# Attention and two Strassen-style products on one core: GpSimd's sums given to VectorE, six places for raw words, another order at pair changes

## The chip, the core and the metric

The kernel runs on one core of a Trainium2 chip. Its engines are TensorE (PE, matmuls; PEld is its weight load), VectorE (DVE), ScalarE (ACT), GpSimd (POOL) and SyncE (SP), which here only issues DMAs; ACT issues DMAs too. Each engine takes its instructions in the order in which they were written. The metric is the device time of one execution in microseconds (us), as the median of several runs.

## The reference, cut to what matters

```python
def _attn_ref(q, k, v, p):             # batch 8, heads 8, seq 576, head_dim 64; 32 packed rows
    p_packed = sm_attn(p, k, v)        # softmax(p k^T / 8) v
    return sm_attn(q, p_packed, p_packed)

def _moe_ref(x, w1, w2, w3, w_out):    # x: 4608 x 512, w1, w2: 512 x 1024
    return ((x @ w1) * (x @ w2)) @ w3 @ w_out

def _moe2_ref(x, w_in, w_out):         # w_in: 512 x 2048, w_out: 2048 x 512
    h = x @ w_in
    g = np.where(h >= 1, h, np.where(h <= -1, 0.0, (h + 1) ** 2 / 4))
    return g @ w_out
```

The output of attention is the input of the first product chain, and that chain's output is the input of the second.

## The kernel before

All big matmuls take each operand as two parts, a high part (an ACT copy into the matmul's own fp32r type) and a remainder (value minus high part, a subtract on DVE or POOL), and make three products of them (`PASSES`). The work has three stages.

**Stage one** (to about 620 us of the trace) does attention and the first chain, batch by batch (`b`). Within a batch, 16 `ab_unit`s (L378) and 8 `x2_unit`s (L402) follow each other on PE; attention of the next batch is spread between them, and after every unit one item of `weight_tasks` (L576) is run, which prepares the weights of the second chain: `convert` turns 64-bit words into float32 (ACT and three DVE instructions), `combine` (L637) adds two 128x512 quarters on POOL, and `part` (L626) makes the high part on ACT and the remainder on POOL and stores both to DRAM.

**Stage two** (about 620 to 1028 us) is x @ w_in as a Strassen-Winograd product with seven products (A11, S1, S2, A12, S4, S3, A22). The columns of x come in five pairs of halves (`PAIRS`): four of 512 columns and a last one of 256. A pair has eight steps `s`; a step runs the seven products of six matmuls on PE, the A22 of a step only after S1 of the next one. ACT copies the bank of A11 to `m1`, of S1 to `m5` and of S2 to `u2`, because S2, S4 and S3 add onto those banks; DVE adds them back (L869: `U` twice, `L` once). `upper` and `lower_*` put the piecewise square on the results (ACT: L809, L812; DVE: L815), and form the differences U2 = U1 - U0 (L837, end of `upper`) and two planes of `L` (`lower_end`, L858); SP stores all to DRAM (`gd`) for stage three. While a pair runs, the seven right sides of the next pair are made by eleven tasks (`x2_tasks`, L662): seven `parts` (ACT copy L672, DVE remainder L673 into one of nine `x2s` tiles) and four `combine`s (POOL, L667, in place in the tile `f`). Tables set where they run: `MID` (after A12 of step i), `LAST` (after S3) and `END` (after `upper`). Before the change, S4 and S3 of the next pair come in END of step 7, and its A22 in END of step 0, that is when that pair already runs.

**Stage three** (from about 1028 us) is g @ w_out in the same scheme: 5 pairs x 7 products x 4 entries `j`. An entry loads a tile of raw words (`raw`, 128x1024 floats for the wide pairs, 512 KB) by SP (L924), makes high part (ACT, L941) and remainder (DVE, L942) in one of five `op` tiles, and PE runs 12 matmuls on it (L1050). An entry of A22 needs two raw tiles, subtracted in place first (`g_combine`, POOL, L933). At entry x the program makes the parts of entry x + 3, fills free raw places with loads (`g_load`), and subtracts for entry x + 5 if that is of A22. There are four raw places (`RAWS`). After the fourth entry of a product `evacuate` takes its two banks out: A11, S1, S2 and A22 by ACT copies (L1023), A12, S3 and S4 by DVE adds (L1027).

```python
    def g_combine(x):
        if x < len(seq) and seq[x][1] == A22:
            a, b = rawg[x]
            nc.gpsimd.tensor_tensor(out=a, in0=a, in1=b, op=ALU.subtract)
...
        g_parts(x + AHEAD)
        g_load()
...
        g_combine(x + AHEAD + 2)
```

The activation's scratch tiles are those of tag `r` ([128, 2, 512], two of them): the relu and its square stand there in stage two, and nothing uses them after it.

## Time and profile before

| | |
|---|---|
| three runs | 1438.79 us median (1434.61 to 1439.05) |
| the profiled execution | 1430.22 us, of it 1428.4 us span from the first to the last instruction |
| PE busy | 1308.1 us (92% of the span) |
| DVE busy | 849.6 us (59%) |
| ACT busy | 676.0 us (47%) |
| POOL busy | 206.7 us (14%) in 134 instructions |
| chain that ended last | PE 53%, DVE 17%, DMA 14%, ACT 9%, POOL 2% |
| granted clock of PE, mean | 0.971 of full speed |

The busy shares are means over three stages with different limits. Of a stretch, read first how long PE was busy in it and at which granted clock, then what its waits ended on. The profiled execution is 8.6 us shorter than the median of the runs. Raw loads were 128 DMAs, right sides' and weights' POOL work stands in stages one and two, and the POOL subtracts of stage three are 20.

### The profile page before, as it was taken

How to read it: one execution, taken by the hardware profiler on the slowest of the kernel's cores; microseconds unless marked ns; L12 is line 12 of the kernel's file. 1: busy time of each engine (PE TensorE's matmuls, PEld its weight loads, DVE VectorE, ACT ScalarE, POOL GpSimd, SP SyncE). 2: the span in 40 equal slices, each digit the busy share in tenths (PEclk: the TensorE clock that was granted, in tenths of full speed). 3: DMA queues.
4: the chain of work that ended last, by engine and by line, in shares of the span. 5: the costliest groups of instructions: out<-in, count | busy, mean ns of one | idle time of the engine just before them, and what ended most of it. 6: DMA issues, size and time to landing. Idle time of an engine off the chain costs nothing.

```text
span 1428.4 us, 21147 instructions
## 1 busy us (share of the span) xinstructions
PE 1308.1 (92%) x8184; PEld 1072.7 (75%) x8184; DVE 849.6 (59%) x1334; ACT 676.0 (47%) x1144; POOL 206.7 (14%) x134
## 2 busy tenths in 40 slices
PE   6689799999999999989989899898879899998988
PEld 2366578879888898968767687787767687877877
DVE  4684576658676766617767777666634544444533
ACT  3344244445545454426656667565533443425333
POOL 0000032333233232201101020000001102020011
PEclk9799999999999999989999999999999999999999
DMA  8763465557555533178566565567898666666665
GB/s 278 233 218 104 143 214 193 173 186 232 200 182 196 203 141 145 50 281 323 211 228 213 206 237 196 207 216 266 275 343 351 240 216 236 220 218 228 223 201 164
DMA packets 122900, 306.78 MB, mean 215 GB/s; under 512 B 10160, under 2 KB 44976, under 8 KB 117680
## 3 DMA queue, kind: packets, MB, share of 16 engines
q1 hardware_dynamic: 85904, 236.09, 47.8%
q10 hardware_dynamic: 36896, 69.35, 13.6%
q8 instruction: 64, 1.05, 0.3%
q14 instruction: 36, 0.29, 0.1%
HBM read 199.36 MB, written 106.04 MB: 214 GB/s over the span
## 4 chain that ended last, share of the span: by engine, by line
PE 53%; DVE 17%; DMA 14%; ACT 9%; issue 4%; POOL 2%; ACTq 1%; SPq 0%; POOLq 0%; DVEq 0%
PE psk L402 11%; PE x L1050 10%; PE psk L378 8%; PE x L801 7%; DMA raw<-g 6%; PE z L801 3%; PE z L1050 3%; PE y L1050 3%; DVE op L942 2%; ACT r L809 2%; ACT r L812 2%; PE psk L486 2%; DMA raw<-w3T 2%; PE y L801 2%; DVE U L815 2%
## 5 line engine op out<-in xcount | busy, mean ns | idle before, releaser
L942 DVE TENSOR_TENSOR op<-raw,op 128x1024 fp32r<-128x1024 f32 (+1 forms) x140 | 161.3, 1188 | 182.8 <-ACT op L941 182.1
L402 PEld LDWEIGHTS psk<-g,w 128*128 128x128 f32 x1500 | 200.3, 188 | 28.4 <-ACT st L429 17.7
L378 PE MATMUL psk<-at,m 128*128 128x288 f32 x1494 | 214.3, 298 | 5.0 <-DVE at L329 1.9
L378 PEld LDWEIGHTS psk<-at,m 128*128 128x128 f32 x1494 | 200.7, 188 | 19.7 <-issue 9.5
L941 ACT ACTIVATE op<-raw 128x1024 fp32r<-128x1024 f32 (+1 forms) x140 | 130.3, 968 | 173.9 <-POOL raw L933 76.8
L402 PE MATMUL psk<-g,w 128*128 128x288 f32 x1500 | 209.1, 297 | 3.8 <-ACT st L429 3.3
L626 POOL TENSOR_TENSOR hl<-cvx,hl 128x512 fp32r<-128x512 f32 x56 | 73.9, 1319 | 447.6 <-ACT hl L625 411.6
L1050 PE MATMUL x<-op,w 128*128 128x512 f32 (+1 forms) x480 | 111.5, 388 | 25.2 <-ACT op L941 13.9
L801 PE MATMUL x<-x2s,wi 128*128 128x512 f32 (+1 forms) x480 | 120.0, 387 | 7.4 <-ACT m L865 6.9
L1050 PEld LDWEIGHTS x<-op,w 128*128 128x128 f32 x480 | 87.5, 197 | 48.5 <-ACT op L941 17.1
L801 PEld LDWEIGHTS x<-x2s,wi 128*128 128x128 f32 x480 | 87.9, 197 | 29.4 <-ACT m L865 10.4
L390 DVE TENSOR_TENSOR tb<-psk,ta 128x288 f32<-128x288 f32 x124 | 56.3, 454 | 86.3 <-ACT ta L388 61.8
L809 ACT ACTIVATE r<-U,half 128x1024 f32<-128x1024 f32 (+1 forms) x40 | 42.7, 1067 | 126.8 <-DVE U L869 126.8
L933 POOL TENSOR_TENSOR raw<-raw,raw 128x1024 f32<-128x1024 f32 (+1 forms) x20 | 43.8, 2190 | 404.6 <-DMA raw<-g 338.6
L667 POOL TENSOR_TENSOR f<-f 128x1024 f32<-128x1024 f32 (+1 forms) x20 | 43.7, 2186 | 361.2 <-DVE x2s L673 360.8
L104 DVE TENSOR_TENSOR g<-tb,g 128x288 fp32r<-128x288 f32 x128 | 91.6, 716 | 3.4 <-ACT g L103 2.8
L815 DVE SCALAR_TENSOR_TENSOR U<-U,r 128x512 f32<-128x512 f32 (+1 forms) x80 | 58.9, 777 | 53.1 <-ACT r L812 53.1
L801 PE MATMUL x<-x2s,ws 128*128 128x512 f32 (+1 forms) x240 | 62.3, 395 | 19.4 <-ACT x2s L672 8.0
L812 ACT ACTIVATE r<-r 128x1024 f32<-128x1024 f32 (+1 forms) x80 | 78.0, 975 | 2.5
L1050 PE MATMUL x<-op,hwi 128*128 128x512 f32 (+1 forms) x360 | 77.3, 373 | 0.0
L486 PE MATMUL psk<-wo,w3f 128*128 128x512 f32 x128 | 62.9, 644 | 13.9 <-DVE w3f L135 13.9
L124 ACT ACTIVATE cvt<-raw 128x512 f32<-128x512 f32 x72 | 48.4, 675 | 54.1 <-DMA raw<-w 25.9
(112 smaller groups left out, 2040.7 us busy)
## 6 DMA issues: line engine op xcount, KB each, us to landing
raw<-g SPq DMA_DIRECT2D x128, 512.0 KB, 4.9
g<-L SPq DMA_DIRECT2D x32, 1024.0 KB, 4.1
ws<-ws ACTq DMA_DIRECT2D x38, 512.0 KB, 4.3
g<-U SPq DMA_DIRECT2D x64, 256.0 KB, 2.0
w<-hl ACTq DMA_DIRECT2D x28, 512.0 KB, 3.0
x2d<-st ACTq DMA_DIRECT2D x72, 144.0 KB, 2.6
wi<-hl ACTq DMA_DIRECT2D x20, 512.0 KB, 5.1
qk<-kT SPq DMA_DIRECT2D x8, 1152.0 KB, 9.1
```

The costliest lines, as they stand in the source:

```text
L104: nc.vector.tensor_tensor(out=dst[:, 1], in0=src, in1=dst[:, 0].bitcast(F32), op=ALU.subtract)
L378: nc.tensor.matmul(ps[w][:, :HS], m_tile[b, w, n][:, s, G, c0 * P:(c0 + 1) * P], at_tile[b][:, G, v, hf * HS:(hf + 1) * HS], start=(k == 0 ...
L402: nc.tensor.matmul(ps, w34[kt][:, s, mt * P:(mt + 1) * P], g_t[kt, hf][:, v, :], start=(kt == kts[0] and n == 0), stop=(kt == kts[-1] and ...
L486: nc.tensor.matmul(acc[4 * hf + m], w3f[hf, j][:, m * P:(m + 1) * P], wof[j], start=(j == 0), stop=(j == 7))
L626: nc.gpsimd.tensor_tensor(out=lo, in0=q[a], in1=hi.bitcast(F32), op=ALU.subtract)
L801: nc.tensor.matmul(bank[s, b][:, :N], w, x2_t[t, q][:, m, k, :N], start=(j == 0 and q in (A11, S1, A12)), stop=(j == 5), skip_group_check= ...
L809: nc.scalar.activation(out=r, in_=h, func=AF.Relu, scale=0.5, bias=half)
L812: nc.scalar.activation(out=r, in_=r, func=AF.Square)
L815: nc.vector.scalar_tensor_tensor(out=out, in0=h, scalar=1.0, in1=r, op0=ALU.max, op1=ALU.min)
L941: nc.scalar.activation(out=o[:, :, 0, :N], in_=a[0], func=AF.Copy)
L942: nc.vector.tensor_tensor(out=o[:, :, 1, :N], in0=a[0], in1=o[:, :, 0, :N].bitcast(F32), op=ALU.subtract)
L1050: nc.tensor.matmul(bank[b][d][:, :N], w2_t[q][j // 2][:, 2 * (j % 2) + k, s, d * P:(d + 1) * P], op[x][:, k, v, :N], start=start and k == ...
```

## The change

Every tensor instruction of POOL goes to DVE, in its place in program order: the 56 remainders and 32 sums of `weight_tasks`, the 20 `combine`s of `x2_tasks` and the 20 of `g_combine`. The raw ring gets six places; the two new ones are the two `r` tiles. The first four entries are loaded as before (`g_load(4)`), the next loads come after the stores of the last step. In `x2_tasks` the last combine writes to quarter 11 instead of 21 and stands ahead of the parts of A12. The subtract that ended `upper` becomes `upper_end`. At a pair change (step 0 of the next pair) the tasks S4, S3 and A22 run after A11, after S1 and after A12 of that step, and `upper_end` and `lower_end` of the step before run only after S3.

```diff
-                    nc.gpsimd.tensor_tensor(out=lo, in0=q[a], in1=hi.bitcast(F32), op=ALU.subtract)
+                    nc.vector.tensor_tensor(out=lo, in0=q[a], in1=hi.bitcast(F32), op=ALU.subtract)
...
-                return lambda: nc.gpsimd.tensor_tensor(out=q[d], in0=q[a], in1=q[b], op=op)
+                return lambda: nc.vector.tensor_tensor(out=q[d], in0=q[a], in1=q[b], op=op)
...
-            return lambda: nc.gpsimd.tensor_tensor(out=x2f[dst], in0=x2f[a], in1=x2f[b], op=ALU.subtract)
+            return lambda: nc.vector.tensor_tensor(out=x2f[dst], in0=x2f[a], in1=x2f[b], op=ALU.subtract)
...
-            parts(S2, 11), parts(A12, 21), combine(21, 21, 11), parts(S4, 22), parts(S3, 12), parts(A22, 21),
+            parts(S2, 11), combine(11, 21, 11), parts(A12, 21), parts(S4, 22), parts(S3, 12), parts(A22, 11),
...
+        store(s, G11, 1, h[:, 0:1, :N])
+
+    def upper_end(s):
+        N = PAIRS[s // 8][1]
+        h = kept[s, 0]
         nc.vector.tensor_tensor(out=h[:, 2, :N], in0=h[:, 1, :N], in1=h[:, 0, :N], op=ALU.subtract)
-        store(s, G11, 1, h[:, 0:1, :N])
         store(s, GT1, 1, h[:, 2:3, :N])
...
-    RAWS, OPS = 4, 5
+    RAWS, OPS = 6, 5
...
     def raw_tile(n):
-        return ring("raw", n, [P, 2, 512], F32)
+        return buf("r") if n > 3 else ring("raw", n, [P, 2, 512], F32)
...
-            nc.gpsimd.tensor_tensor(out=a, in0=a, in1=b, op=ALU.subtract)
+            nc.vector.tensor_tensor(out=a, in0=a, in1=b, op=ALU.subtract)
...
-    MID = {2: 2, 3: 1, 4: 1, 5: 1, 7: 1}
+    MID = {2: 2, 3: 1, 4: 1, 5: 1, 7: 1, 0: 1}
     LAST = {7: 2}
-    END = {7: 2, 0: 1}
...
         if s:
             lower_begin(s - 1)
+        tasks(1 if i == 0 else 0)
         product(s, S1)
...
             ws_load(s + 1, nc.scalar)
+        tasks(1 if i == 0 else 0)
         product(s, S2)
...
-        if s:
+        if s and i:
             lower_end(s - 1)
...
+        if s and i == 0:
+            upper_end(s - 1)
+            lower_end(s - 1)
         tasks(LAST.get(i, 0))
         if s + 1 < steps:
             upper(s)
-            tasks(END.get(i, 0))
+            if i < 7:
+                upper_end(s)
...
-            for n in range(RAWS):
+            for n in range(4):
                 tiles["raw", n] = raw_tile(n)
-            g_load()
+            g_load(4)
...
     lower_end(steps - 1)
     flush_stores()
+    g_load()
```

What this does to the order of instructions is shown at three places. Names are those of the program; a number behind one tells buffers apart, and x, y, z are PE's banks.

The first is ACT in step 0 of the second pair, the pair change (`m` is m1 or m5, `u` is u2, `x2s` a right side). Before, from the square of step 7's `upper` on:

```order
L812 ACTIVATE r<-r 128x1024
L672 ACTIVATE x2s<-f 128x1024 x2
L865 ACTIVATE m_8526<-x 128x512
L809 ACTIVATE r<-L,half 128x512
L865 ACTIVATE m_8537<-z 128x512
L809 ACTIVATE r<-x,half 128x512
L812 ACTIVATE r<-r 128x1024
L752 DMA ws<-ws_74 128x1024
L865 ACTIVATE u_8557<-x 128x512
L809 ACTIVATE r<-U,half 128x1024
L812 ACTIVATE r<-r 128x1024
L672 ACTIVATE x2s<-f 128x1024
```

ACT in the same place after the change:

```order
L812 ACTIVATE r<-r 128x1024
L869 ACTIVATE m_8518<-x 128x512
L809 ACTIVATE r<-L,half 128x512
L672 ACTIVATE x2s<-f 128x1024
L869 ACTIVATE m_8532<-z 128x512
L809 ACTIVATE r<-x,half 128x512
L812 ACTIVATE r<-r 128x1024
L752 DMA ws<-ws_74 128x1024
L672 ACTIVATE x2s<-f 128x1024
L869 ACTIVATE u_8555<-x 128x512
L672 ACTIVATE x2s<-f 128x1024
L809 ACTIVATE r<-U,half 128x1024
```

The copies for S4 and S3 moved from ahead of m1 to behind it, one of them ahead of m5 and one ahead of u2; the copy for A22 moved from behind `upper` of step 0 to ahead of it.

The second is DVE in step 2 of the first pair, where the program makes the first right side of the next pair (L673, remainder) and the first combine. Before:

```order
L869 TENSOR_TENSOR U<-y,m_7441 128x512
L858 TENSOR_TENSOR L<-L,U 128x1024
L673 TENSOR_TENSOR x2s<-f,x2s 128x1024
L869 TENSOR_TENSOR U<-z,u_7472 128x512
L869 TENSOR_TENSOR L<-x,m_7452 128x512
```

DVE in the same place after the change:

```order
L873 TENSOR_TENSOR U<-y,m_7441 128x512
L862 TENSOR_TENSOR L<-L,U 128x1024
L673 TENSOR_TENSOR x2s<-f,x2s 128x1024
L667 TENSOR_TENSOR f<-f 128x2x512
L873 TENSOR_TENSOR U<-z,u_7472 128x512
L873 TENSOR_TENSOR L<-x,m_7452 128x512
```

The combine, POOL's before, now stands on DVE ahead of the two adds that take PE's banks.

The third is DVE around the A22 entries of the second pair in stage three (`U<-z` and `L<-x` are `evacuate` of S4 and S3). Before:

```order
L1027 TENSOR_TENSOR L<-x,L 128x512 x2
L942 TENSOR_TENSOR op_11290<-raw_11222,op_11290 128x2x512
L942 TENSOR_TENSOR op_11307<-raw_11240,op_11307 128x2x512
L942 TENSOR_TENSOR op_11327<-raw_11272,op_11327 128x2x512
L942 TENSOR_TENSOR op_11347<-raw_11310,op_11347 128x2x512
L1027 TENSOR_TENSOR U<-z,U 128x512 x2
L942 TENSOR_TENSOR op_11369<-raw_11330,op_11369 128x2x512
L942 TENSOR_TENSOR op_11389<-raw_11350,op_11389 128x2x512
```

DVE in the same place after the change (`r` is a raw place in an activation's scratch tile):

```order
L1038 TENSOR_TENSOR L<-x,L 128x512 x2
L946 TENSOR_TENSOR op_11294<-raw_11190,op_11294 128x2x512
L937 TENSOR_TENSOR raw_11242<-raw_11242,raw_11244 128x1024
L946 TENSOR_TENSOR op_11311<-raw_11207,op_11311 128x2x512
L937 TENSOR_TENSOR r<-r 128x1024
L946 TENSOR_TENSOR op_11331<-raw_11242,op_11331 128x2x512
L937 TENSOR_TENSOR raw_11314<-raw_11314,raw_11316 128x1024
L946 TENSOR_TENSOR op_11351<-r,op_11351 128x2x512
L937 TENSOR_TENSOR raw_11334<-raw_11334,raw_11336 128x1024
L1038 TENSOR_TENSOR U<-z,U 128x512 x2
L946 TENSOR_TENSOR op_11373<-raw_11314,op_11373 128x2x512
L946 TENSOR_TENSOR op_11393<-raw_11334,op_11393 128x2x512
```

The four subtracts of raw words (L937, POOL's L933 before) now stand between the remainders, each two entries ahead of the remainder that uses it, all of them ahead of the two adds that empty S4's banks.

## Rows read from the trace of the kernel before

**Rows 1.** Busy time by stretch: us, engines' busy time, PEclk, DMA share, GB/s

```profile
core 0: us, PE busy (x) PEld busy (x) DVE busy (x) ACT busy (x) POOL busy (x), PEclk, DMA share, GB/s
180.00:606.00 426.00, 414.09 (x3787) 368.44 (x3786) 291.20 (x538) 209.93 (x481) 128.25 (x92) 1.00 0.51 176
705.00:990.00 285.00, 264.19 (x1130) 211.09 (x1129) 198.23 (x267) 177.62 (x240) 26.74 (x13) 0.96 0.62 217
1100.00:1428.00 328.00, 299.81 (x1414) 245.80 (x1412) 147.03 (x142) 122.34 (x150) 43.80 (x20) 0.98 0.64 216
713.00:726.00 13.00, 9.96 (x42) 7.38 (x40) 10.83 (x13) 8.88 (x12) 2.35 (x1) 1.00 0.48 162
```

**Rows 2.** Waits of PE from 1100 us on: us in total, times, longest

```profile
PE x L1050 <- ACT op L941: 13.9, 9, 3.8
PE x L1050 <- DVE op L942: 11.2, 12, 2.4
```

**Rows 3.** The same from 1100 to 1125 us, the first A22 run

```profile
PE x L1050 <- DVE op L942: 4.5, 2, 2.4
PE x L1050 <- ACT op L941: 2.5, 2, 1.6
```

**Rows 4.** Timeline of the third A22 run: start, us, engine, [idle before <-releaser]

```profile
1276.39 1.06 ACT L941 ACTIVATE op<-raw 128x1024 fp32r<-128x1024 f32 x1 [7.92 <-POOL raw L933]
...
1285.84 2.34 POOL L933 TENSOR_TENSOR raw<-raw,raw 128x1024 f32<-128x1024 f32 x1 [6.97 <-DMA raw<-g]
...
1289.32 0.49 PE L1050 MATMUL x<-op,w 128*128 128x512 f32 x1 [3.78 <-ACT op L941]
```

**Rows 5.** The page's DMA issues: count, KB, median us from issue to landing

```profile
raw<-g SPq DMA_DIRECT2D x128, 512.0 KB, 4.9
```

**Rows 6.** Waits of PE from 705 to 990 us, the four pair changes

```profile
PE x L801 <- ACT x2s L672: 8.0, 4, 2.5
PE x L801 <- ACT m L865: 6.2, 6, 1.5
PE x L801 <- DVE x2s L673: 6.2, 4, 1.7
```

**Rows 7.** Timeline of the first pair change, ACT and PE

```profile
713.29 1.99 ACT L672 ACTIVATE x2s<-f 128x1024 fp32r<-128x1024 f32 x2
...
715.81 1.66 PE L801 MATMUL x<-x2s,wi 128*128 128x512 f32 x6 [1.52 <-ACT m L865]
...
718.43 0.58 ACT L865 ACTIVATE u<-x 128x512 f32<-128x512 f32 x1
...
720.12 1.56 PE L801 MATMUL x<-x2s,wi 128*128 128x512 f32 x6
...
726.31 0.50 PE L801 MATMUL x<-x2s,ws 128*128 128x512 f32 x1 [1.83 <-ACT x2s L672]
...
728.55 2.50 PE L801 MATMUL x<-x2s,ws 128*128 128x512 f32 x5 [1.74 <-DVE x2s L673]
```

**Rows 8.** Timeline, steps 2, 3 and 5 of the second pair

```profile
746.92 1.22 DVE L673 TENSOR_TENSOR x2s<-f,x2s 128x1024 fp32r<-128x1024 f32 x1
...
750.93 0.58 ACT L865 ACTIVATE m<-x 128x512 f32<-128x512 f32 x1
...
751.77 1.56 PE L801 MATMUL x<-x2s,wi 128*128 128x512 f32 x6
...
771.70 1.67 PE L801 MATMUL x<-x2s,wi 128*128 128x512 f32 x6 [0.17 <-ACT m L865]
```

**Rows 9.** DVE groups by form, 180 to 606 us: count, busy us, mean ns, idle before

```profile
L104 DVE TENSOR_TENSOR g<-tb,g 128x288 fp32r<-128x288 f32 x112 | 84.4, 754 | 0.0
L390 DVE TENSOR_TENSOR tb<-psk,ta 128x288 f32<-128x288 f32 x112 | 50.8, 454 | 72.3 <-ACT ta L388 55.5 <-PE psk L378 10.0 <-ACT g L103 6.5
L104 DVE TENSOR_TENSOR m<-psk,m 128x512 fp32r<-128x512 f32 x50 | 32.2, 685 | 31.4 <-ACT m L103 31.4
```

**Rows 10.** The page's costliest groups: POOL's remainders of weights in stage one

```profile
L626 POOL TENSOR_TENSOR hl<-cvx,hl 128x512 fp32r<-128x512 f32 x56 | 73.9, 1319 | 447.6 <-ACT hl L625 411.6
```

More of the change, by code (lines that the diff above doesn't have):

```diff
@@ L1006, in fused_kernel @@
     upper(steps - 1)
+    upper_end(steps - 1)
     lower_begin(steps - 1)
```

## Prediction

> **What bounds the kernel now.** First the busy time by stretch [rows 1]. In 180 to 606 us, most of stage one, PE is busy 414 of 426 us at a granted clock of 1.00: there is little to win. In the pair changes of stage two (705 to 990 us) it is busy 264 of 285 us at 0.96, and from 1100 us on 300 of 328 us at 0.98. So the sum is made of what PE loses in these two stretches, by standing still and by running at the lower of its two clock levels (1.2 of 2.4 GHz).
>
> Next who PE waits for. From 1100 us on it waits 13.9 us for high parts and 11.2 us for remainders [rows 2], 25.1 us, all at the entries of A22 (five runs of four); 7.0 us of it in the first run [rows 3]. The timeline of the third run shows why [rows 4]: POOL's subtract had been waiting for a raw load, ACT for POOL, PE for ACT. The lower clock costs 328 x 0.02 = 6.6 us more. In stage two PE waits 8.0 + 6.2 + 6.2 = 20.4 us at four pair changes [rows 6]. The first change shows the three stops [rows 7]: 1.52 us at S2 of step 0 (ACT copied two right sides from 713.29 us, m1 came behind them), 1.83 and 1.74 us at A22 (its right side is made behind `upper`). That is 5.1 us a change. The clock costs 285 x 0.04 = 11.4 us.
>
> **Part 1, A22 in stage three.** An entry of A22 holds two raw places, so with four places two entries are on their way. One needs a load of 4.9 us [rows 5], POOL's 2.34 us and ACT's 1.06 us [rows 4], and a DVE remainder of 1.22 us (same shape in [rows 8]): 9.5 us for two entries, 4.8 us each. PE needs 2.9 us for twelve matmuls: three products of six took 4.31 us from 715.81 to 720.12 [rows 7]. With six places three entries are on their way, and the subtract takes DVE's 1.22 us: 4.9 + 1.22 + 1.06 + 1.22 = 8.4 us for three, 2.8 us each. That is just under PE's pace, so I let the stops of the three middle runs go entirely. In the first run the loads share the DMA engines with stage three's weights; I keep 3 of its 7.0 us. In the last run entries are half as long, but a load is not half as quick; I keep 1.3 us. Gain 25.1 - 4.3 = 20.8 us, with ends at 12 (half of it) and 25.1. Of the 6.6 us of low clock I count 5 as gained, since a run that stops for 3 us may still have it.
>
> The change adds a wait: DVE now waits for the raw load itself. Behind the subtract for entry x + 5 stand the remainder of the entry ahead of it and, at the fourth subtract, the two adds that empty S4's banks; PE waits for both. The third A22 entry can be loaded only when the remainders of S4's last two entries free its places, so DVE stands about 3 us there. What hides this is the two finished `op` tiles that PE then still has, 2 x 2.9 = 5.8 us. Without that cover it would cost those 3 us in each of five runs, 15 us.
>
> **Part 2, the pair change.** ACT has ten instructions from `upper` of step 7 to u2 in either order, so u2 still ends near 719.0 us (718.43 + 0.58, [rows 7]). m1 now comes where the copies began, at 713.29 us, so S2 can start on time, at 715.81 - 1.52 = 714.3 us, and S3 three products later, at 718.6 us. But S3 needs u2 and its right side's remainder. The copy for that now comes just ahead of u2 and ends about 718.4 us; on DVE the two `smaller` of the old pair (0.69 us each, [rows 9]) stand in front, then the remainder takes its 1.22 us: it ends between 719.7 and 720.4 us. S3 started at 720.12 us before. So the first stop isn't gained, it moves from S2 to S3 (1.1 to 2.2 us). A22's right side is ready by then, and A22 starts three products behind S3: the two later stops, 3.57 us, go. Three changes: 10.7 us. At the fourth the new products have 256 columns while ACT and DVE still work on 512 of the old pair; I count 1.3 of its 5.1 us. `upper_end` and `lower_end` of step 7 come later, behind the adds; their stores have a step of time until their buffers are needed, so I cost that at nothing; if the stores were late, DVE's add would wait about 1 us a change.
>
> **Part 3, inside a pair.** Four combines of 1.22 us a pair go from POOL to DVE. In step 2 the remainder ends at 748.1 us, then come the add, `upper` and m1, which ends at 751.51 us; S2 starts at 751.77 [rows 8]. The slack is 0.26 us, and a combine of 1.14 us (1.22 less the overlap of neighbours) stands now between: a stop of 0.9 us. ACT then runs late, and each of the next three tasks adds about 0.5 us; one of them shows 0.17 us already [rows 8]. That is 2.2 us a pair, for three pairs 6.6 us lost; the fourth prepares a pair of half the width, where I see none.
>
> **The clock in stage two.** Of its 11.4 us I take 9 as additional to the stops, and give back 7.5, because the stops that remain are shorter and stand alone: in 713 to 726 us, where the only stop was 1.52 us, the clock stayed at 1.00 [rows 1, 7]. The ends are 0 and 9.
>
> **Part 4, stage one.** 88 instructions of POOL (56 of 1.32 us [rows 10], 32 sums alike) become DVE instructions of 0.69 us [rows 9]: 60.7 us. But POOL's work slows DVE. The remainder of g, with both inputs in SBUF, takes 754 ns on average; the product of the same length just before it, with an input in PSUM, takes 454 ns [rows 9]. That is 112 x 0.30 = 33.6 us which come back. DVE goes from 291 to 318 of 426 us, 75%. I count 0 us, between 3 us of gain (stretched instructions in PE's path get shorter) and 22 us of loss (below). The Trainium skill, "SBUF — State Buffer", section "SBUF: two separate sides", says that a GpSimd instruction and a DVE one with two SBUF inputs exclude each other, the loser blocked for the whole instruction. By it alone every POOL instruction could hold up DVE for its 1.3 us, 88 x 1.3 = 114 us, and DVE would have less to do after the change; by the row it has 27 us more. The measured 33.6 us stays.
>
> **The sum.** Stage three 20.8 + 5; stage two 10.7 + 1.3 - 6.6 + 7.5; stage one 0: 38.7 us. The profiled execution takes 1430.2 us, so 1391.5 us; it lies 8.6 us under the median of the runs, to which the same gain is applied: 1438.8 - 38.7 = 1400 us.
>
> **The rivals.**
> *Stage two gives nothing.* The moved stop at S3 and the stops inside the pairs keep the clock low (7.5 us not gained) and come out twice as long (6.6 us more): 1414 us. For it: a moved stop of about 2 us is longer than the 1.52 us that left the clock alone.
> *DVE waits for loads in stage three.* If raw loads need more than the cover, the 15 us above are paid and the clock's 5 with them: 1420 us. For it: [rows 5] is a median over quiet and crowded stretches. Against it: DMA is busy 0.64 there [rows 1].
> *Slower: DVE becomes the bound of stage one.* Place: the `ab_unit`s, where PE's banks are emptied by DVE's product and a remainder now stands in DVE's queue waiting for ACT's copy. It decides once DVE's idle time there, 135 of 426 us, no longer absorbs the 60.7 us, and nothing of POOL's slowing comes back. Then 60.7 - 38.7 = 22 us of loss: 1461 us. Against it: 68% busy. The Trainium skill, "Perfetto Trace Analysis", section "Optimizing Scalar/DVE Operations", speaks for this one: where DVE is saturated, giving work to other engines, even GpSimd, may make sense. By the row DVE isn't saturated.
> *The change doesn't do what it says.* If the two scratch tiles come free late, stage three has four places still, and only POOL's 1.1 us an entry are won: about half of 25.8 us, 1413 us.
>
> **How the numbers follow.** The forecast, 1392 to 1408 us, gets 0.50; better than that (nearly all stops and low clock gone, 1384 to 1392 us) 0.06; the first rival 0.22, the second 0.10, the third 0.06, the last 0.03; 0.03 is left for the first two rivals with a loss of some us in stage one, which would leave no change. The range reaches from 1388 to 1424 us: below to half of the better case, above over the first, second and last rival; left out are 0.06 for the third, 0.03 for no change, and some 0.08 at the two ends. A measurement of this kernel can tell 0.3%, about 4 us, from no change. Faster 0.91, within that 0.03, slower 0.06.
>
> **What would show it.** Stage three right: PE's waits at A22 fall from 25.1 to about 4 us, and none is left in the middle runs. The pair change right: no wait at A22, one of 1.1 to 2.2 us at S3. Inside a pair: waits of 0.5 to 0.9 us for m1 in steps 3 to 6. Stage one right: remainders of g at about 450 ns, PE's busy time as before. Wrong: DVE's subtracts idle on DMA while PE waits for remainders; a granted clock in stage two not above 0.96; a longer stage one.

## The result and the profile after

| | before | after |
|---|---|---|
| median of the runs side by side | 1438.92 us (1434.61 to 1439.82) | 1388.37 us (1387.34 to 1389.97) |
| profiled execution, its span | 1430.22 us, 1428.4 | 1387.40 us, 1385.6 |
| stage one | 623.5 us | 616.8 us |
| stage two | 404.5 us | 395.8 us |
| stage three | 400.4 us | 373.0 us |

The ratio is 0.9655, 95% interval 0.9633 to 0.9678. 1388.4 us lies 0.4 us inside the lower end of the range that was given (1388 to 1424 us), 12 us under the forecast; two of the four runs lie just below that end. The stages are cut at PE's first matmul on a right side of stage two (`x2s`) and at its first on an `op` tile; every stage length below is taken in this way from the trace of the run named.

The first view is the page of the kernel after: the busy line and the chain that ended last, by engine.

```profile
PE 1295.8 (94%) x8184; PEld 1065.7 (77%) x8184; DVE 879.6 (63%) x1462; ACT 674.8 (49%) x1144; POOL 0.7 (0%) x6
...
PE 55%; DVE 16%; ACT 13%; DMA 10%; issue 5%; SPq 1%; ACTq 1%; DVEq 0%
```

POOL's 206.7 us are gone and DVE's 849.6 have grown to only 879.6 us: DVE took over 128 instructions and is busy 30 us longer. PE still works through the same 8184 matmuls. In the chain, DMA has fallen from 14% to 10%.

The busy time by stretch, as in [rows 1] (us, engines' busy time, clock, DMA share, GB/s); the third stretch is shorter, since the kernel ends earlier:

```profile
core 0: us, PE busy (x) PEld busy (x) DVE busy (x) ACT busy (x) POOL busy (x), PEclk, DMA share, GB/s
180.00:606.00 426.00, 419.52 (x3832) 374.41 (x3831) 309.25 (x630) 213.97 (x484) 0.00 (x0) 1.00 0.52 176
705.00:990.00 285.00, 270.96 (x1224) 217.66 (x1224) 207.92 (x301) 182.43 (x256) 0.00 (x0) 0.98 0.65 230
1100.00:1380.00 280.00, 277.61 (x1352) 232.58 (x1351) 146.44 (x153) 115.75 (x145) 0.00 (x0) 0.99 0.68 233
```

From 1100 us on PE is busy 277.6 of 280 us, against 300 of 328 in [rows 1]; in stage one 419.5 of 426 against 414.1. The clock in the pair changes is 0.98 against 0.96.

Waits of PE from 1010 us on (us in total, times, longest), which answer to [rows 2]:

```profile
PE z L1061 <- ACT op L945: 7.2, 1, 7.2
PE x L1061 <- DVE op L946: 6.7, 4, 3.1
```

The second line is all that is left of the 25.1 us at A22. The four stops stand at 1090.9 and 1099.7 us (1.26 and 3.06 us, first run), 1335.1 us (1.07, fourth run) and 1379.1 us (1.31, last run); none is left in the second and third run. The first line is a stop that was there before (6.8 us, at the start of the stage, on bank z).

The first pair change, timeline of DVE, ACT and PE, which answers to [rows 7]:

```profile
714.31 0.58 ACT L869 ACTIVATE u<-x 128x512 f32<-128x512 f32 x1
714.70 1.22 DVE L673 TENSOR_TENSOR x2s<-f,x2s 128x1024 fp32r<-128x1024 f32 x1
...
714.94 0.50 PE L801 MATMUL x<-x2s,wi 128*128 128x512 f32 x1 [0.62 <-ACT u L869]
...
715.97 1.43 PE L801 MATMUL x<-x2s,wi 128*128 128x512 f32 x5 [0.54 <-DVE x2s L673]
...
717.24 1.56 PE L801 MATMUL x<-x2s,wide 128*128 128x512 f32 x6
718.64 1.56 PE L801 MATMUL z<-x2s,wi 128*128 128x512 f32 x6
720.04 1.56 PE L801 MATMUL x<-x2s,ws 128*128 128x512 f32 x6
```

The stop sits at S3, first for u2 and then for the right side's remainder, 1.16 us together; A11 and S1 of the next step (717.24 and 718.64 us) and A22 (720.04 us) follow without one.

Steps 3 and 4 of the second pair (steps are counted from 0), where DVE still has the combines of steps 2 and 3 in its queue; DVE, ACT, PE and its weight load (PEld):

```profile
737.44 1.22 DVE L667 TENSOR_TENSOR f<-f 128x1024 f32<-128x1024 f32 x1
738.24 1.56 PE L801 MATMUL z<-x2s,wi 128*128 128x512 f32 x6
738.58 0.68 DVE L873 TENSOR_TENSOR U<-z,u 128x512 f32<-128x512 f32 x1
...
739.30 1.15 ACT L809 ACTIVATE r<-U,half 128x1024 f32<-128x1024 f32 x1 [3.58 <-DVE U L873]
739.92 1.23 PEld L801 LDWEIGHTS x<-x2s,ws 128*128 128x128 f32 x6 [0.56 <-DVE L L873]
739.92 1.67 PE L801 MATMUL x<-x2s,ws 128*128 128x512 f32 x6
...
741.45 0.58 ACT L869 ACTIVATE m<-x 128x512 f32<-128x512 f32 x1
...
742.08 1.67 PE L801 MATMUL x<-x2s,wi 128*128 128x512 f32 x6 [0.50 <-ACT m L869]
...
743.59 1.56 PE L801 MATMUL y<-x2s,wi 128*128 128x512 f32 x6
...
750.59 1.56 PE L801 MATMUL x<-x2s,ws 128*128 128x512 f32 x6
752.41 1.66 PE L801 MATMUL x<-x2s,wi 128*128 128x512 f32 x6 [0.26 <-ACT m L869]
753.91 1.56 PE L801 MATMUL y<-x2s,wi 128*128 128x512 f32 x6
```

The combine stands ahead of DVE's add of U, ACT's relu waits for that add, m1 comes behind the relu, and S2 at 742.08 us waits for m1. Read the starts here, not only the idle time. Undisturbed products start 1.40 us apart (749.18, 750.59). Around the stop of 0.26 us the distances are 1.82 and 1.50 us, so it costs 0.52 us, twice what its row says. Around the first one they are 1.68, 2.16 and 1.51 us: 1.15 us, of which PE's row shows 0.50. The first 0.28 us of it lie ahead of that stop: A22 at 739.92 us starts late behind DVE's add of L, which only the row of its weight load shows. The stop of 0.50 us itself costs 0.87 us.

DVE's groups by form from 180 to 606 us (count, busy us, mean ns, idle before), which answer to [rows 9, 10]:

```profile
L390 DVE TENSOR_TENSOR tb<-psk,ta 128x288 f32<-128x288 f32 x112 | 50.7, 453 | 23.5 <-ACT ta L388 12.3 <-PE psk L378 7.7 <-ACT g L103 3.0
L104 DVE TENSOR_TENSOR g<-tb,g 128x288 fp32r<-128x288 f32 x112 | 50.2, 448 | 0.0
```

The remainder of g has fallen from 754 to 448 ns with its own shape unchanged: 34.3 us, for 33.6 forecast.

The last pair, DVE and PE, where the kernel before had no such stop:

```profile
978.94 0.42 DVE L873 TENSOR_TENSOR L<-x,m 128x256 f32<-128x256 f32 x1 [6.03 <-DMA g<-L]
...
979.42 1.65 PE L801 MATMUL x<-x2s,ws 128*128 128x256 f32 x6 [5.20 <-DVE L L873]
```

DVE's add may not overwrite `L` before a store has read it, and PE waits for that add.

### The profile page after: what moved, and what is told of

Same layout as the page of the kernel before. It is cut to its first block, busy times and chain, and to the rows that moved or that the text cites. A ratio compares the mean times of both kernels' runs of the same rounds, so it can differ in the third digit from the quotient of the medians.

```text
span 1385.6 us, 21076 instructions
## 1 busy us (share of the span) xinstructions
PE 1295.8 (94%) x8184; PEld 1065.7 (77%) x8184; DVE 879.6 (63%) x1462; ACT 674.8 (49%) x1144; POOL 0.7 (0%) x6
## 4 chain that ended last, share of the span: by engine, by line
PE 55%; DVE 16%; ACT 13%; DMA 10%; issue 5%; SPq 1%; ACTq 1%; DVEq 0%
PE x L1061 13%; PE psk L402 12%; PE psk L378 9%; PE z L1061 5%; ACT r L809 5%; ACT r L812 4%; PE y L1061 4%; PE x L801 3%; DVE U L873 2%; PE psk L486 2%; DMA raw<-g 2%; PE psk L194 2%; DMA raw<-w3T 2%; ACT m L869 2%; DVE L L815 2%
## 5 line engine op out<-in xcount | busy, mean ns | idle before, releaser
L402 PEld LDWEIGHTS psk<-g,w 128*128 128x128 f32 x1500 | 200.8, 189 | 25.7 <-ACT st L429 16.5
L946 DVE TENSOR_TENSOR op<-raw,op 128x1024 fp32r<-128x1024 f32 (+1 forms) x94 | 101.0, 1112 | 63.3 <-ACT op L945 63.3
L945 ACT ACTIVATE op<-raw 128x1024 fp32r<-128x1024 f32 (+1 forms) x94 | 86.5, 965 | 83.0 <-DVE L L1038 31.9
L801 PEld LDWEIGHTS x<-x2s,wi 128*128 128x128 f32 x480 | 84.4, 192 | 36.1 <-ACT m L869 12.4
L1061 PE MATMUL x<-op,w 128*128 128x512 f32 (+1 forms) x480 | 102.6, 373 | 6.7 <-DVE op L946 6.7
L946 DVE TENSOR_TENSOR op<-r,op 128x1024 fp32r<-128x1024 f32 (+1 forms) x46 | 50.0, 1116 | 52.3 <-ACT op L945 52.2
L390 DVE TENSOR_TENSOR tb<-psk,ta 128x288 f32<-128x288 f32 x124 | 56.2, 453 | 38.2 <-ACT ta L388 19.4
L486 PE MATMUL psk<-wo,w3f 128*128 128x512 f32 x128 | 63.9, 652 | 13.9 <-DVE w3f L135 13.7
L815 DVE SCALAR_TENSOR_TENSOR U<-U,r 128x512 f32<-128x512 f32 (+1 forms) x80 | 47.4, 634 | 46.1 <-ACT r L812 46.1
L1061 PEld LDWEIGHTS x<-op,hwi 128*128 128x128 f32 x360 | 62.7, 188 | 13.1
L801 PE MATMUL x<-x2s,ws 128*128 128x512 f32 (+1 forms) x240 | 58.7, 381 | 10.3 <-DVE L L873 9.9
L945 ACT ACTIVATE op<-r 128x1024 fp32r<-128x1024 f32 (+1 forms) x46 | 43.0, 968 | 47.9 <-DVE L L1038 17.2
L388 ACT ACTIVATE ta<-psk 128x288 f32<-128x288 f32 x125 | 50.3, 402 | 28.5 <-PE psk L378 26.9
```

The lines of the kernel that those rows point to most:

```text
L388: nc.scalar.activation(out=bs, in_=ps[1][:, :HS], func=AF.Copy)
L390: nc.vector.tensor_tensor(out=g, in0=ps[0][:, :HS], in1=bs, op=ALU.mult)
L402: nc.tensor.matmul(ps, w34[kt][:, s, mt * P:(mt + 1) * P], g_t[kt, hf][:, v, :], start=(kt == kts[0] and n == 0), stop=(kt == kts[-1] and ...
L486: nc.tensor.matmul(acc[4 * hf + m], w3f[hf, j][:, m * P:(m + 1) * P], wof[j], start=(j == 0), stop=(j == 7))
L801: nc.tensor.matmul(bank[s, b][:, :N], w, x2_t[t, q][:, m, k, :N], start=(j == 0 and q in (A11, S1, A12)), stop=(j == 5), skip_group_check= ...
L815: nc.vector.scalar_tensor_tensor(out=out, in0=h, scalar=1.0, in1=r, op0=ALU.max, op1=ALU.min)
```

## The experiments

All times are medians of the runs, with their ratio to the kernel before where several runs stand behind it. The column of low clock is half of the time for which the clock's records show the lower of the two levels: what that level costs where PE works through it, and more than it costs where PE stands still in that time.

| kernel | median us | ratio, interval | stage one | two | three | low clock, two / three |
|---|---|---|---|---|---|---|
| before | 1438.9 | 1 | 623.5 | 404.5 | 400.4 | 17.1 / 11.1 |
| before, again | 1440.8 (one run) | | 624.5 | 404.6 | 409.9 | 17.1 / 19.8 |
| after | 1388.4 | 0.9655 [0.9633, 0.9678] | 616.8 | 395.8 | 373.0 | 8.5 / 5.1 |
| weights on DVE alone | 1433.5 | 0.9955 [0.9928, 0.9982] | 620.1 | 405.2 | 411.8 | 17.1 / 20.8 |
| six places alone, POOL | 1400.4 | 0.9723 [0.9685, 0.9761] | 624.8 | 405.2 | 368.6 | 13.7 / 3.6 |
| raw subtracts on DVE alone | 1459.7 | 1.0141 [1.0094, 1.0188] | 623.9 | 405.2 | 428.2 | 17.1 / 27.3 |
| six places and DVE | 1399.4 (one run) | | 620.8 | 404.5 | 372.4 | 17.0 / 5.1 |
| new order alone | 1423.7 | 0.9887 [0.9848, 0.9926] | 629.3 | 389.2 | 404.9 | 8.5 / 17.4 |
| combines on DVE alone | 1433.7 (one run) | | 621.2 | 406.4 | 404.3 | 11.9 / 17.9 |
| after, combines later | 1380.8 | 0.9607 [0.9562, 0.9652] | 617.8 | 387.7 | 372.1 | 11.9 / 5.6 |
| after, raw and sides on POOL | 1378.5 | 0.9590 [0.9558, 0.9623] | 617.0 | 389.6 | 370.8 | 8.5 / 7.1 |
| after, raw on POOL, combines later | 1377.2 | 0.9583 [0.9547, 0.9618] | 618.6 | 390.1 | 370.6 | 10.1 / 5.1 |
| that, S2's weights later | 1370.6 | 0.9545 [0.9518, 0.9572] | 612.0 | 388.7 | 364.3 | 8.5 / 1.7 |
| that, A11's weights later too | 1366.2 | 0.9498 [0.9469, 0.9526] | 616.0 | 383.1 | 366.8 | 10.2 / 3.8 |

Stage one contains the first loads, whose time varies by some us from run to run (620.8 to 629.3 us among kernels that have stage one unchanged). Where stage one matters, the length behind PE's stop near 162 us is used, from which on the traces run alike.

### Stage one: the weights' work on DVE alone

```diff
-                    nc.gpsimd.tensor_tensor(out=lo, in0=q[a], in1=hi.bitcast(F32), op=ALU.subtract)
+                    nc.vector.tensor_tensor(out=lo, in0=q[a], in1=hi.bitcast(F32), op=ALU.subtract)
...
-                return lambda: nc.gpsimd.tensor_tensor(out=q[d], in0=q[a], in1=q[b], op=op)
+                return lambda: nc.vector.tensor_tensor(out=q[d], in0=q[a], in1=q[b], op=op)
```

> The kernel before with the 88 weight sums and remainders of stage one on DVE, nothing else. Theory: GpSimd was in DVE's way (the remainder of g took 754 ns on average, 450 ns alone), so stage one alone gives the 6.6 us that it is shorter in the changed kernel: its end (first matmul on a right side) goes from 623.5 to about 617 us, stages two and three stay at 404.5 and 400.4 us, 7 us faster in all. Rival: the added 60 us on DVE eat that up and the 6.6 us come from elsewhere: no change within 2 us.

Behind 162 us stage one took 455.2 us, against 461.0 before and 454.5 in the full change: 5.8 of 6.5 us come from this edit. It does not hang on one trace: the seven traces with the weights' work on POOL have 460.3 to 463.2 us there, the seven with it on DVE 453.0 to 456.5. The median fell by 5.2 us, for 7 expected. DVE's groups from 180 to 606 us in this kernel:

```profile
L104 DVE TENSOR_TENSOR g<-tb,g 128x288 fp32r<-128x288 f32 x112 | 56.1, 501 | 0.0
L390 DVE TENSOR_TENSOR tb<-psk,ta 128x288 f32<-128x288 f32 x112 | 50.6, 452 | 22.3 <-ACT ta L388 12.4 <-PE psk L378 7.7 <-ACT g L103 1.8
```

The remainder of g takes 501 ns instead of 754, and the stops of PE between 165 and 612 us fall from 14.3 us (14 stops) to 8.6 (11); in the full change they are 8.2. So POOL's work did delay PE through DVE, but not through the remainder of g, whose mean changed most: the stops that shrank end on other work. One of the two longest of them shows the path, in the kernel before (293 to 301 us) and, below it, in this one (295 to 302 us):

```profile
296.53 1.29 POOL L626 TENSOR_TENSOR hl<-cvx,hl 128x512 fp32r<-128x512 f32 x1 [7.94 <-DMA x2d<-st]
...
296.94 1.50 DVE L315 TENSOR_TENSOR big<-big,qsm 128x576 f32<-128x576 f32 x1
...
299.28 0.68 ACT L328 ACTIVATE at<-big 128x576 fp32r<-128x576 f32 x1 [2.58 <-DVE big L318]
...
300.31 0.92 PE L402 MATMUL psk<-g,w 128*128 128x288 f32 x5 [1.66 <-ACT st L429]
```

```profile
297.65 0.76 DVE L315 TENSOR_TENSOR big<-big,qsm 128x576 f32<-128x576 f32 x1
...
300.29 1.88 PE L402 MATMUL psk<-g,w 128*128 128x288 f32 x12 [0.61 <-ACT st L429]
```

DVE's product L315, with both inputs in SBUF, took 1.50 us beside POOL's remainder and 0.76 us without it; a transpose of DVE, two copies of ACT (L328 and L429) and PE stand behind it, and PE's stop shrinks from 1.66 us to 0.61. The other stops were not followed like this. The Trainium skill, "SBUF — State Buffer", section "SBUF: two separate sides", lets GpSimd and a DVE instruction with two SBUF inputs exclude each other. The trace agrees that such DVE instructions, and not those with a PSUM input (L390: 454 and 452 ns), get shorter when POOL is empty.

### Stage three: places, and the engine of the raw subtract

Six places, nothing else (the two new ones in the scratch tiles, as in the change):

```diff
-    RAWS, OPS = 4, 5
+    RAWS, OPS = 6, 5
...
+        return buf("r") if n > 3 else ring("raw", n, [P, 2, 512], F32)
```

> The kernel before with six raw places, the subtract of raw words left on GpSimd. Theory: the places are what counts; three entries on their way at 4.9 + 2.34 + 1.06 + 1.22 = 9.5 us are 3.2 us each against 2.9 us of PE, so PE's waits at A22 fall from 25 to 3 to 6 us and stage three goes from 400 to 376 to 380 us. Rival: GpSimd's slower subtract, which also blocks DVE while it runs, keeps half of the stops: stage three 388 us or more.

Stage three took 368.6 us, 4.4 less than in the full change, and less than the 376 to 380 us expected: the low clock went with the stops (3.6 us, for 11.1 before). PE's waits from 1028 us on, on `op` tiles:

```profile
PE x L1051 <- DVE op L942: 3.0, 4, 2.1
...
PE x L1051 <- ACT op L941: 0.3, 1, 0.3
```

The subtract on DVE, nothing else (four places):

```diff
-            nc.gpsimd.tensor_tensor(out=a, in0=a, in1=b, op=ALU.subtract)
+            nc.vector.tensor_tensor(out=a, in0=a, in1=b, op=ALU.subtract)
```

> The kernel before with the subtract of raw words on DVE, four raw places left. Theory: the chain of an entry gets 1.1 us shorter for two entries on their way (4.2 us each, PE 2.9), and DVE waiting for loads costs something: stage three 390 to 397 us, 3 to 10 us faster. Rival: with so few places the load lands so late that DVE's wait holds up the remainders and adds behind it: no gain or up to 10 us slower.

This is slower than before by 1.4%, as the rival of the expectation had it: stage three took 428.2 us. Waits from 1028 us on:

```profile
DVE raw L933 <- DMA raw<-g: 72.1, 17, 7.7
PE x L1050 <- DVE op L942: 39.5, 12, 5.4
```

DVE stands 72.1 us waiting for raw loads in front of its subtracts, with remainders and the adds that free banks queued behind, and PE waits 39.5 us for those remainders. On POOL nothing but the next subtract stands in the queue behind such a wait; on DVE, what PE needs does. That was the rival of the prediction in which DVE waits for loads: with four places it holds.

Both edits together, all else as before:

```diff
-    RAWS, OPS = 4, 5
+    RAWS, OPS = 6, 5
...
-            nc.gpsimd.tensor_tensor(out=a, in0=a, in1=b, op=ALU.subtract)
+            nc.vector.tensor_tensor(out=a, in0=a, in1=b, op=ALU.subtract)
```

> The kernel before with six raw places and the raw subtracts on DVE, all else as before. With six places and POOL's subtracts stage three took 368.6 us, in the changed kernel, with DVE's, 373.0. Theory: the 4.4 us are the price of the subtract on DVE; stage three takes 372 to 375 us here too. Rival: they come from the new order in stage two, which hands stage three its first entries later; then stage three takes 368 to 370 us here. Stages one and two as before (about 624 and 405 us).

Stage three took 372.4 us, so the theory holds: of the 4.4 us by which the full change lies above six places with POOL, 3.8 are there with DVE's subtract alone. These are one trace each, and the whole times (1400.4 us, and 1399.4 in one run) do not tell the kernels apart, since stage one came out 4.0 us shorter here. But the eight traces with six places agree: the five runs of A22, each with the A11 behind it, take 96.3 to 99.5 us in the five with POOL's subtract and 99.7 to 100.9 in the three with DVE's. Waits from 1028 us on:

```profile
DVE raw L933 <- DMA raw<-g: 20.2, 8, 5.9
PE x L1051 <- DVE op L942: 6.7, 4, 3.0
```

Six places cut DVE's waiting from 72.1 to 20.2 us. With POOL the places bring stage three, 400.4 to 411.8 us in five traces, down to 368.6; with DVE from 428.2 to 372.4. The Trainium skill, "Perfetto Trace Analysis", section "Optimizing Scalar/DVE Operations", sees a use for giving DVE's work to GpSimd where DVE is saturated. Here POOL is 3.8 us better with DVE busy half of the time (142.2 of 280 us from 1100 us on in the kernel with six places and POOL), which fits the waits above: what counts is in whose queue the wait for the load stands. On that point the measurement decides.

### The kernel before, again

No edit.

> The kernel before, unchanged, for a second trace. The trace on record took 1430.2 us, 8.6 us less than the median. Theory: stage three, whose stops at A22 bring the low clock with them, is what differs from run to run; the traces with its old scheme so far show 400.4, 404.9 and 411.8 us. So here too stage three is longer than 400.4 us (404 to 412), and stages one and two are within 2 us of 623.5 and 404.5 us. Rival: all stages are longer in proportion.

Stages one and two are the same within 1.0 us, and stage three took 409.9 us instead of 400.4. PE's waits on `op` tiles from 1025 us on:

```profile
PE x L1050 <- ACT op L941: 14.7, 8, 3.7
PE x L1050 <- DVE op L942: 13.1, 12, 2.6
```

The stops come to 27.8 us against 25.1 [rows 2], but half the time at the low clock is 19.8 instead of 11.1 us. The two differences, 2.7 and 8.7 us, are together more than the 9.5, since PE stands still in some of that time; the clock is the larger part. Why it fell more often here isn't known. In this trace and in those of three more kernels that leave stage three's four places and POOL as they were, that half is 17.4 to 20.8 us. The trace on which the prediction was made was thus one with a short stage three.

### Stage two: order and combines

The new order of tasks and ends alone, POOL keeps all its work and there are four places (the edits of order in the change, none of the others):

```diff
+        tasks(1 if i == 0 else 0)
         product(s, S1)
...
+        tasks(1 if i == 0 else 0)
         product(s, S2)
...
+        if s and i == 0:
+            upper_end(s - 1)
+            lower_end(s - 1)
```

> The kernel before with the new order at pair changes alone, all GpSimd work left there. Theory: the order takes away the stops at A22 (3.6 us a change) and with them the low clock of stage two, and the stops of 0.3 to 0.5 us inside the pairs, which come from combines on DVE, are not there: stage two goes from 404.5 to 390 to 394 us. Rival: with GpSimd's combines DVE is held up at the change itself, and the gain is no more than the 8.7 us of the full change: 396 us or more.

Stage two took 389.2 us, 15.3 less than before. PE's waits for m1 and m5 from 640 to 950 us, in this kernel and, below it, in the kernel after:

```profile
PE x L801 <- ACT m L869: 0.4, 2, 0.2
```

```profile
PE x L801 <- ACT m L869: 3.9, 12, 0.5
```

The stops inside the pairs belong to the combines on DVE: 395.8 - 389.2 = 6.6 us. The rows show 3.5 us of that; the rest lies in the longer distances of products around each stop, as above. An undisturbed step takes 9.80 us from its A11 to the next one; with the combines on DVE steps 3 to 6 of the second pair take 10.95, 10.32, 10.32 and 10.32 us, with those on POOL 9.88, 9.80, 10.18 and 9.80.

The combines on DVE in the old order:

```diff
-            return lambda: nc.gpsimd.tensor_tensor(out=x2f[dst], in0=x2f[a], in1=x2f[b], op=ALU.subtract)
+            return lambda: nc.vector.tensor_tensor(out=x2f[dst], in0=x2f[a], in1=x2f[b], op=ALU.subtract)
```

> The kernel before with the combines of right sides on DVE, in the old order. In the new order the combines on DVE cost stage two 6.6 us (395.8 against 389.2 us). Theory: they delay the adds that free PE's banks and with them m1, whatever the order at pair changes: stage two takes 409 to 413 us, 4 to 8 us more than before (404.5). Rival: in the old order the stops at pair changes set the end and hide the delay, or POOL's own slower combines had cost as much: 403 to 406 us. Stages one and three as before (624, and 400 to 412 us).

Stage two took 406.4 us, 1.9 more than before and between the two expectations. PE's waits from 620 to 1030 us:

```profile
PE x L801 <- ACT m L865: 10.2, 17, 1.6
PE x L801 <- DVE x2s L673: 6.2, 4, 1.8
PE x L801 <- ACT x2s L672: 5.4, 4, 2.5
```

The stops for m1 are there (17 of them, 10.2 us; 9 of 7.4 us in the kernel before, again), but the stops for right sides are 2.6 us shorter and the low clock costs 11.9 instead of 17.1 us. The starts of A11 take the two apart. Steps 3 to 6 of the second pair take 10.95, 10.32, 10.33 and 10.33 us here, as in the new order, so inside the pairs the theory holds: the combines cost the same in either order. At the pair changes the next steps (step 1 of the second, third and fourth pair) take 13.1, 14.6 and 13.1 us, for 16.3, 15.5 and 16.6 before and 15.3, 16.5 and 15.5 in the kernel before, again, which hides it, as the rival had it. Why the clock fell less there is not settled by this one run.

The combines behind the adds, otherwise the kernel after:

```diff
-    MID = {2: 2, 3: 1, 4: 1, 5: 1, 7: 1, 0: 1}
-    LAST = {7: 2}
+    MID = {2: 1, 4: 1, 7: 1, 0: 1}
+    LAST = {2: 1, 3: 1, 5: 1, 7: 2}
```

> The changed kernel with the combines of steps 2, 3 and 5 moved from behind A12 to behind S3, so that on DVE they stand behind the two adds that take PE's banks. Theory: the stops of 0.5 and three times 0.26 us inside a pair are DVE's combines ahead of those adds; they go, and stage two goes from 395.8 to 390 to 392 us, the 389.2 us that the same order gave with the combines on GpSimd. Rival: the 6.6 us between the two come from something else that DVE's combines cost; then stage two stays at 394 to 396 us.

Stage two took 387.7 us, 8.1 less than in the kernel after, and the stops for m1 between 640 and 950 us are down to one of 0.3 us. That is more than the 6.6 us, since step 5 of three pairs, at 10.2 us a little long in the old order too, takes 9.80 us now. The cost of the combines was their place in DVE's queue and not DVE's time.

Two versions that give work back to POOL: the kernel after with raw subtracts and combines on POOL, and with raw subtracts on POOL and the combines later on DVE. Against the kernel after, both have the first edit and the former alone the second; the latter has the tables of the run above:

```diff
-            nc.vector.tensor_tensor(out=a, in0=a, in1=b, op=ALU.subtract)
+            nc.gpsimd.tensor_tensor(out=a, in0=a, in1=b, op=ALU.subtract)
...
-            return lambda: nc.vector.tensor_tensor(out=x2f[dst], in0=x2f[a], in1=x2f[b], op=ALU.subtract)
+            return lambda: nc.gpsimd.tensor_tensor(out=x2f[dst], in0=x2f[a], in1=x2f[b], op=ALU.subtract)
```

> The changed kernel with the combines of right sides and the subtracts of raw words back on GpSimd; the weights' work stays on DVE, six places and the new order stay. Theory: the parts add up: stage one as in the changed kernel (454.5 us behind its 5.7 us wait), stage two 389 to 390, stage three 368 to 369 us: 10 to 12 us less than the changed kernel's 1385.6 us span. Rival: GpSimd blocking DVE costs in the new order what the combines on DVE cost: no gain over the changed kernel.

> The changed kernel with the subtracts of raw words back on GpSimd and the combines of right sides on DVE behind the adds. Theory: stage two 390 to 392 us, stage three 368 to 369 us, 9 to 11 us less than the changed kernel. Rival: stage three stays at 373 us, because what costs there is the first run, whose loads share the DMA engines with weights, on whichever engine the subtract is.

They took 1378.5 and 1377.2 us, with stage two at 389.6 and 390.1 and stage three at 370.8 and 370.6 us. Against each other they are the same, and both gain some 10 us on the change as it was made. In stage three POOL's subtract gains 2.2 us (370.8 for 373.0) and 1.5 (370.6 for 372.1), less than the 3.8 in the old order (368.6 for 372.4), so both miss the 368 to 369 us expected by some 2 us.

### Two stops on transfers

In the version with raw subtracts on POOL and later combines, the stop at the start of stage three is 7.5 us. The edit moves one load:

```diff
-    w2_load(S2)
     upper(steps - 1)
...
     flush_stores()
     g_load()
+    w2_load(S2)
```

> The changed kernel with raw subtracts on GpSimd and the combines behind the adds (as in the run of that version, 1377 us), and with one more move: the load of stage three's weights for S2 is issued behind the first four raw loads instead of ahead of them. Theory: PE's stop of 7.2 to 7.5 us at the start of stage three is a raw load that stands behind those weights on the DMA engines; with the weights behind it the stop shrinks to 2 to 4 us, and the time falls by 2 to 6 us, to 1371 to 1375 us. Rival: the first pair of stage three is bound by what it loads in all, weights and raw words; then the stop only moves to a later entry (S2 waiting for its weights, or the first run of A22), and the time stays at 1377 us within 2 us.

PE's waits from 1000 us on:

```profile
PE x L1061 <- DVE op L946: 3.1, 3, 2.0
PE z L1061 <- ACT op L945: 1.8, 1, 1.8
PE x L1061 <- ACT op L945: 1.4, 2, 1.2
```

The stop on z is 1.8 us instead of 7.5 and does not come back later: 3.1 and 1.4 us are all that is left at A22, and stage three is 6.3 us shorter. The median fell by 6.6 us, a little more than expected; the intervals of the two ratios overlap, so it is the stop that shows the effect and not the median.

Last, A11's weights of stage three, which the kernel loads in step 1 of the last pair:

```diff
-        if s == 8 * len(PAIRS) - 7:
+        if s == 8 * len(PAIRS) - 5:
             w2_tile(A11, late["f"], "f")
             w2_load(A11)
```

The page on DMA of the kernel after shows what they meet there, from 955 to 985 us (KB each, median us from issue to landing):

```profile
w<-w SPq DMA_DIRECT2D x2, 1024.0 KB, 10.8
g<-L SPq DMA_DIRECT2D x3, 512.0 KB, 7.1
```

> The version with S2's weights of stage three behind the raw loads (1370.6 us), and with the weights of A11 for stage three (two loads of 1024 KB) issued two steps later, behind step 3 of the last pair instead of behind step 1. In the changed kernel a stop of 5.2 us that the kernel before did not have stands in step 2 of the last pair: DVE's add waits 6.0 us for a store of L, while these weights are on the DMA engines, and a second of 3.9 us stands two steps later, as before. Theory: the first stop is the collision of the stores with those weights; moved, it is gone (under 1.6 us), the second one grows by 0 to 3 us, stage two falls from 388.7 to 384 to 387 us and the time by 2 to 5 us. Rival: the short steps of the last pair store and load more than the DMA engines move in their time in any order; then the stop only moves to step 4 or to the start of stage three, and stage two and three together stay at 753 us within 2 us.

PE's waits on `L` from 930 to 1040 us, in the version without and, below it, with this edit:

```profile
PE x L801 <- DVE L L873: 10.9, 3, 5.6
```

```profile
PE x L801 <- DVE L L873: 6.4, 2, 5.3
```

One of the two long stops is gone. Without the edit they stood in steps 3 and 6 of the last pair (5.6 and 4.5 us, behind the adds of steps 2 and 5); with it one stands in step 5 (5.3 us), two steps later, as the weights are. So the stop goes where those weights go; whether it is the first one moved, with the second gone, or the second one come earlier, the rows don't say. The last pair is 5.3 us shorter (56.6 for 61.9 us), stage two 5.6 shorter, stage three 2.5 longer, and the median 4.4 us shorter, with intervals that overlap. This version has the lowest median of all: 1366.2 us, 22 us under the change as it was made.

## Why the prediction was right, and where its sum was off

On the profiled executions the forecast was 38.7 us and the gain 42.8: stage one +6.7 for 0, stage two 8.7 for 12.9, stage three 27.4 for 25.8. The misses partly cancel, and the median gained 7.7 us more than the profile (below). That put the time among the 1384 to 1392 us that had 0.06, and not for the reason given there, that nearly all stops and low clock go: 6.7 us of stops at A22 stayed, and of the low clock a half of 8.5 and 5.1 us. The mechanisms of stages two and three were forecast in the main; that the time stayed inside the range, by 0.4 us, is luck.

**Stage three, right in kind and size.** The stops at A22 fell from 25.1 to 6.7 us (18.4 for 20.8 forecast) and the low clock's cost from 11.1 to 5.1 us (6.0 for 5); the remaining 3.0 us of the 27.4 are not taken apart. By the starts of the products the gain is where it was forecast: the five runs of A22, each with the A11 behind it, take 100.9 us for 127.2, 26.4 of the 27.4 us. In the first run 4.3 us stayed for 3 forecast, in the last 1.3 for 1.3, and the fourth kept 1.07 where none was expected. DVE's added wait is real (20.5 us in eight waits in the kernel after, 20.2 with six places and DVE alone), and six places keep most of it from PE; the 6.7 us that PE waits for remainders are what the prediction named as a sign of being wrong, in small. But one step failed: the subtract's move from POOL to DVE was put down as a gain of 1.1 us an entry. It is a loss, of 1.5 to 4 us with six places (one trace each) and of 16 to 28 us with four (428.2 against 400.4 to 411.8). So the rival "four places still", priced at half of the gain, would have come out on the slower side.

**The pair change, right.** A stop of 1.16 us at S3 (1.1 to 2.2 forecast), none at A22, and half the time at the low clock in stage two is 8.6 us less (7.5 forecast). By the starts of A11 the first two steps of the second, third and fourth pair are 19.3 us shorter together, clock included, for 10.7 + 7.5 forecast.

**Inside a pair, right in sum.** The rows show 0.50 and three times 0.26 us where 0.9 and 0.5 were forecast, but by the starts of A11 the steps are 1.15 and 0.52 us longer, and the comparison with the new order alone gives 6.6 us, as the sum had it.

**The fourth change, mis-sized.** 1.3 us were counted as gained. From the point where S2 of the last pair's first step is due until stage three begins, the kernel before took 54.8 us and the kernel after 58.2: 3.4 us lost. The new order alone has it too: its last pair takes 61.5 us, the kernel after 61.1, the kernel before 57.7. PE comes earlier into the short steps, and there the stores meet A11's weights; a new stop of 5.20 us takes back what the change gave, and with the weights moved one of the two long stops goes. These 4.7 us are more than the 4.2 by which stage two fell short. The prediction looked at engines there, but not at what an earlier PE runs into.

**Stage one, mis-sized.** The term was 0, with 3 us as the most that could be gained, and 6.7 us came (6.5 behind the first 162 us). The 33.6 us that DVE gets back were right (34.3), and DVE's 309 of 426 us are under the 318 forecast. The step that failed is the last one: the balance of DVE's busy time was taken as the measure, although PE's stops there were never set by it. They shrank from 14.3 to 8.2 us. The one that was followed came from a single instruction in PE's path that took longer while POOL ran (L315, 1.50 for 0.76 us; 1038 for 759 ns on average), as the prediction's 3 us of gain had it; only the size was off. The rival in which DVE becomes the bound of stage one is ruled out.

**From the profile to the median.** The same gain was taken off the median, 8.6 us above the profiled execution. That execution had the shortest stage three of the five traces with the old scheme (400.4 us, for 404.3 to 411.8), with half of its low clock at 11.1 us where another had 19.8 with nearly the same stops. What six places remove is larger in the others: against the kernel before, again, stage three gains 36.9 us and not 27.4. These 9.5 us are enough for the step of 7.7 us, from 42.8 us to the 50.5 between the medians.

## What to carry to other kernels

In this kernel an instruction that waits for a transfer was better on an engine with nothing else in its queue, though that engine takes twice as long for it (2.34 for 1.22 us), and the buffers were worth far more than the choice of engine. Price a short stop by the starts of the products around it and not by its idle row, and price work on a shared engine by its place in the queue, not by its busy time: the same combine cost 6.6 us ahead of the adds and nothing behind them. Where an edit lets the main engine arrive earlier, look up which transfers stand at the new time, and hold several traces against the median before a gain is taken from one.

## What was not expected of the hardware

A stop of PE of 0.26 us cost 0.52 us, and one of 0.50 us 0.87, by the starts of neighbouring products that otherwise stand 1.40 us apart. The same kernel with nearly the same stops in stage three (25.1 and 27.8 us) had 11.1 us as half of its time at the lower clock level in one execution and 19.8 in another. A DVE instruction with both inputs in SBUF took 754 ns on average in a stage in which POOL worked 30% of the time and 448 ns when it did not work, and PE felt such delays (L315) although DVE was busy only 68% of the time.
